# The first unit's projections in plain f32, earlier branch hints, and the last stores from ScalarE, in a gated-linear-attention plus mixture-of-heads kernel

## The chip, the cores and the metric

The kernel runs on 1 core of one Trainium2 chip. The metric is the device time of one execution in microseconds (us). Before the change the median of three runs is 321.53 us.

## The reference, cut to what matters

Two layers run one after the other. The first is gated linear attention over 4 batches, 8 heads, 768 steps, head size 48; its output, transposed, is the input `x` of the second, an attention with four experts.

```python
for t in range(S):                         # S = 768, per batch and head, state is 48 x 48
    state = alpha[:, :, t, :, None] * state + np.einsum('bhd,bhe->bhde', k[:, :, t], v[:, :, t])
    y[:, :, t] = np.einsum('bhd,bhde->bhe', q[:, :, t], state)
x = y.transpose(0, 2, 1, 3).reshape(B, S, H * D)         # 4 x 768 x 384
logits = x @ w_gate                        # top 2 of 4 experts, softmax of their logits: w
for e in range(E):                         # 4 experts, 64 columns each
    q, k, v = x @ wq[e], x @ wk[e], x @ wv[e]
    a = causal_softmax(q @ k.T / sqrt(64))
    out += (weight of e, 0 where not chosen) * (a @ v @ wo[e])
```

## The kernel before

**Chunks and units.** The first layer works on 24 chunks of 128 steps (six to a batch). For chunk `n`, VectorE runs two scans over alpha (`prep_r`, `prep_c`: the products of alpha from the chunk's end and from its start) and scales k and q by them. TensorE then forms k times q for the 8 heads (`gla_a`, L528), ScalarE or VectorE copies that out of PSUM under a causal mask (tile `ms`), TensorE transposes k (`gla_t`, L555) and adds to the state (`gla_u`, L573), and `gla_y` (L619) makes the chunk's output, already transposed, in PSUM. `check(n)` lets ScalarE take the sum of squares of alpha's products (L510); it guards against overflow. Three chunks are a unit `u` (384 rows of x); there are 8 units.

**Two f32r halves.** The second layer multiplies each operand as a pair of f32r tensors, a rounded one and the remainder: `xh`, `xl` for x, `wqk_h`, `wqk_l` and so on for the weights. ScalarE writes the first by a copy, VectorE the second by a subtraction, and each product is three matmuls. The weights arrive raw in two tiles of the pool `at` (`wqk`; `wv` and `wo` share one), which attention uses later, and are split once (`split_hi`, `split_lo`).

**Projections.** For the units 1 to 7, `proj` (L652) makes q and k of a pair of experts for all 384 columns at once. The first unit is done chunk by chunk instead, so that TensorE has work early: `projp` (L869) for 128 columns of q and of k (18 matmuls), `vproj` (L672) for v and the gate logits (9 matmuls). Then come scores (`score`, L730), softmax on VectorE and ScalarE, `norm` on GpSimd (L767), transposes (`transp`, L785), a times v (`av`, L822) and the output product (`outp`, L848), whose copy ScalarE makes (tile `ot`, L854) and whose store SyncE issues (L856).

**What sets the order.** `Plan.op` records every step with its engine, a modelled duration and its reads and writes. `Plan.schedule` places the steps by a list scheduler: of the steps that could start about now on an engine it takes the one that stands first in the table `TURN`, on TensorE preferring one that keeps the array's tiling (`MODE`: rows halved, columns split, or the full array). `Plan.emit` then writes them out, so each engine's order is fixed when the kernel is built. In the gaps that the plan sees before the array's first full load, `warm` (L1078) inserts dummy matmuls.

**The end.** A flag `cnt`, known long before the end, tells whether the overflow guard held. At the end every engine loads it and branches past a second, exact program that is not run. A hint to the instruction fetcher stands on each engine behind its anchor, the last step that started more than `HINT` = 9 us ahead of the plan's end (only steps whose function returns an instruction can be anchors):

```python
            if x is not None and o["start"] < self.end - HINT:
                self.anchor[o["eng"]] = x
...
        with tc.issue_after(pl.anchor[x].ins):
            tc.mark_branch_hint_location("exact", "LikelyTaken", [e.engine])
    good = nc.values_load(cnt, min_val=0, max_val=P * NG, skip_runtime_bounds_check_because="a count of P * NG flags")
    with tc.If(good < P * NG, label="exact"):
```

Of the kernel before, what the change touches and what calls it, by code (L numbers as in the profile page):

```python
# [56 lines left out]
HINT = 9.0  # L57
TURN = (
# [24 lines left out]
)  # L83
MS_ACT = 3
PIECE = 0.066
QB = 3
N128 = 0.066
# [7 lines left out]
class Plan:  # L95
# [180 lines left out]
    def emit(self, warm=None):  # L276
        pe, warming = ISSUE, True
        for i in self.order:
# [8 lines left out]
            if x is not None and o["start"] < self.end - HINT:  # L287
                self.anchor[o["eng"]] = x
# [3 lines left out]
def tile_gla_moe(ctx: ExitStack, tc: tile.TileContext, qk_d, al_d, v_d, wqk_d, wv_d, wo_d, nat_d, vn_d, out_d):  # L292
# [83 lines left out]
    def build(pl, first_pass):  # L376
        op = pl.op

# [220 lines left out]
        def gla_y(n):  # L599
# [23 lines left out]
            if not first:  # L623
                r += whole(("S", n))
            op("PE", occ, occ + 0.17, f, r=r, pe="py",
               w=whole(("py", n)), use=[("xh", u), ("xl", u)])
# [10 lines left out]
            op("V", *vec(384), fl, r=whole(("py", n)) + [(("xh", u), g)], w=[(("xl", u), g)])  # L637

# [19 lines left out]
        def split(src, c0, n, key, d0, part):  # L658
            cs, ds = slice(c0, c0 + n), slice(d0, d0 + n)
            op("A", *act(n), lambda T: A.activation(T(key)[:, 0, ds], T(src)[:, cs], AF.Copy),  # L660
               r=whole(src), w=[(key, (0, part))])
            op("V", *vec(n), lambda T: V.tensor_tensor(T(key)[:, 1, ds], T(src)[:, cs], T(key)[:, 0, ds].bitcast(F32),
                                                       OP.subtract),
               r=[(src, None), (key, (0, part))], w=[(key, (1, part))])

        def vproj(u, i):
            def f(T):
# [522 lines left out]
```

## Time and profile before

| | us |
|---|---|
| median of 3 runs (lowest, highest) | 321.53 (321.21, 327.66) |
| the profiled execution, its own time | 321.4 |
| its span, first to last instruction | 319.7 |
| TensorE busy | 309.8 (97%) |
| VectorE busy | 242.2 (76%) |
| ScalarE busy | 229.1 (72%) |
| GpSimd busy | 120.2 (38%) |

The profiled execution is 0.1 us below the median, and 1.7 us of it lie outside the span. Busy TensorE time counts each matmul from its start to a modelled end, so neighbours overlap and waits shorter than a matmul's tail don't show. PE is TensorE (PEld its weight loads), DVE VectorE, ACT ScalarE, POOL GpSimd, SP SyncE; a q behind a name is its sequencer.

### The profile page before, as it was taken

To read this page: it belongs to the slowest core of one execution; us is meant where nothing else is said; L and a number is where in the kernel's file an instruction comes from. 1 tells how busy PE (TensorE), PEld (TensorE's weight loads), DVE (VectorE), ACT (ScalarE), POOL (GpSimd) and SP (SyncE) were. 2 spreads that over 40 slices of the span, in tenths; PEclk is the share of its full clock that TensorE was granted. 3 is DMA by queue.
4 is the path that set the end of the run, shared out by engine and by line. 5 is a ranking of instruction groups with operands and counts; after the bars stand their busy time and mean duration, and the time that the engine had idled before them with its cause. 6 is when DMAs were issued, how large, how long until landed. Compare 5 with 4: busy or idle time off the path is not lost. (4 is left out here: it accounts for less than half of the span.)

```text
span 319.7 us, 9830 instructions
## 1 busy us (share of the span) xinstructions
PE 309.8 (97%) x3861; PEld 275.3 (86%) x3861; DVE 242.2 (76%) x708; ACT 229.1 (72%) x594; POOL 120.2 (38%) x177
## 2 busy tenths in 40 slices
PE   8989999999999999999999999999999999999991
PEld 6779998979999879898989899798899978888791
DVE  5999879999999999989999978447674364269430
ACT  0967567867799946869759969577785687669851
POOL 5253206504516510454805452501742060506420
PEclk9999999999999999999999999999999999999998
DMA  7998616313633084312333330240000100010201
GB/s 187 334 255 224 205 54 177 118 72 102 211 101 107 6 247 141 91 51 86 101 111 101 98 92 3 92 139 28 3 2 27 49 3 3 25 49 3 75 29 57
DMA packets 14198, 30.82 MB, mean 96 GB/s; under 512 B 1664, under 2 KB 4960, under 8 KB 14144
## 3 DMA queue, kind: packets, MB, share of 16 engines
q1 hardware_dynamic: 14144, 30.12, 31.4%
q8 instruction: 32, 0.52, 0.7%
q14 instruction: 22, 0.18, 0.2%
HBM read 25.39 MB, written 4.72 MB: 94 GB/s over the span
## 5 line engine op out<-in xcount | busy, mean ns | idle before, releaser
L767 POOL TENSOR_SCALAR a<-a,cf,gw 128x128 f32<-128x128 f32 (+5 forms) x96 | 77.9, 826 | 64.9 <-DVE cf L761 23.1
L748 ACT ACTIVATE a<-a,mx 128x128 f32<-128x128 f32 (+5 forms) x96 | 63.4, 664 | 11.0 <-DVE mx L739 10.9
L739 DVE CUSTOM_DVE_ANT_0 a<-g,cm 128x384 f32<-128x384 f32 (+3 forms) x96 | 47.0, 528 | 5.7 <-PE g L730 4.1
L799 ACT ACTIVATE at<-g 128x512 f32<-128x512 f32 (+3 forms) x124 | 48.8, 463 | 1.7 <-PE g L785 1.4
L785 PE MATMUL g<-ident,a 128*128 128x128 f32 x336 | 45.4, 276 | 0.0
L785 PEld LDWEIGHTS g<-ident,a 128*128 128x128 f32 x336 | 37.9, 141 | 3.1 <-issue 1.2
L822 PE MATMUL g<-at,vg 128*64 128x384 f32 (+2 forms) x324 | 39.5, 391 | 0.0
L730 PE MATMUL g<-k,q 64*128 64x256 f32 (+3 forms) x384 | 37.0, 331 | 0.0
L544 POOL TENSOR_SCALAR_AFFINE_SELECT ms<-ms 128x512 f32<-128x512 f32 x27 | 21.8, 815 | 38.6 <-ACT ms L540 38.3
L822 PEld LDWEIGHTS g<-at,vg 128*64 128x64 f32 x324 | 22.4, 137 | 15.9 <-issue 10.8
L619 PE MATMUL g<-ms,vt 128*32 128x128 f32 x768 | 33.0, 274 | 0.0
L730 PEld LDWEIGHTS g<-k,q 64*128 64x128 f32 x384 | 29.5, 185 | 3.1 <-issue 0.5
L467 DVE TENSOR_TENSOR_SCAN al<-al,d1r 112x516 f32<-112x516 f32 (+1 forms) x25 | 30.5, 1224 | 1.6 <-POOL mask L433 1.6
L590 POOL TENSOR_TENSOR C<-C,ev 112x192 f32<-112x192 f32 x16 | 11.0, 688 | 50.9 <-DVE C L588 49.6
L490 DVE TENSOR_TENSOR_SCAN al<-al,d1c 112x516 f32<-112x516 f32 (+1 forms) x25 | 30.1, 1207 | 0.0
L652 PE MATMUL g<-xh,wqk_h 128*128 128x384 f32 x84 | 29.9, 356 | 0.0
L510 ACT ACTIVATE al<-al 112x1033 f32<-112x1033 f32 x24 | 25.7, 1071 | 4.2 <-DVE qk L498 1.9
L652 PE MATMUL g<-xh,wqk_l 128*128 128x384 f32 x84 | 28.3, 336 | 0.0
L652 PE MATMUL g<-xl,wqk_h 128*128 128x384 f32 x84 | 28.2, 336 | 0.0
L528 PE MATMUL g<-qk 48*128 48x128 f32 x384 | 26.0, 279 | 0.0
L528 PEld LDWEIGHTS g<-qk 48*128 48x128 f32 x384 | 23.2, 187 | 1.7 <-issue 0.7
L619 PE MATMUL g<-qk,S 112*32 112x128 f32 x480 | 24.2, 272 | 0.0
(100 smaller groups left out, 682.0 us busy)
## 6 DMA issues: line engine op xcount, KB each, us to landing
qk<-in_qk_dram SPq DMA_DIRECT2D x24, 448.0 KB, 4.2
vt<-in_v_dram SPq DMA_DIRECT2D x25, 256.0 KB, 4.2
al<-in_al_dram SPq DMA_DIRECT2D x24, 226.2 KB, 3.3
out_dram<-ot SPq DMA_DIRECT2D x24, 192.0 KB, 1.9
at<-in_wqk_dram SPq DMA_DIRECT2D x1, 768.0 KB, 9.0
qk<-in_qk_dram SPq DMA_DIRECT2D x2, 224.0 KB, 4.1
at<-in_wvg_dram SPq DMA_DIRECT2D x1, 390.0 KB, 7.6
at<-in_wo_dram SPq DMA_DIRECT2D x1, 384.0 KB, 9.3
```

The lines of the kernel that those rows point to most:

```text
L467: V.tensor_tensor_scan(backwards(al[0:P, AW + c0 - 1:AW + c1 - 1]), backwards(al[0:P, c0:c1]), d1r[0:P, sl].rearrange("p a w -> p (a w)"), ...
L490: V.tensor_tensor_scan(c, c, T(("d1c", n))[0:P, sl].rearrange("p a w -> p (a w)"), 0.0, OP.mult, OP.max)
L528: PE.matmul(T(("pa", n, s))[:, C * p:C * p + C], t[r:r + D, p, C:2 * C], t[r:r + D, p, 0:C], start=True, stop=True, tile_position=(r, 0))
L619: PE.matmul(py[32 * j:32 * j + 32, k], l, r, start=(i == 0), stop=(i == len(parts) - 1), tile_position=(0, 32 * j))
L652: PE.matmul(pj[:, :W3], w[:, kt, cs], x[:, kt, :], start=(i == 0), stop=(i == 8))
L730: PE.matmul(T(sk[e])[:, :w], q[r, x, ts], k[r, y, c0:c1], start=(m == 0), stop=(m == 2), tile_position=(64 * e, 0))
L739: V.tensor_tensor_reduce(T(ak[e])[:, c0:c1], T(sk[e])[:, :w], cm[:, m0:m0 + w], -1.0, mx[:, 0:1] if x else BIG, OP.add, OP.min, accum_out= ...
L748: A.activation(a[:, 0:n], a[:, 0:n], AF.Exp, bias=T(mk)[:, e, len(pieces) - 1:len(pieces)], scale=-1.0, accum_out=T(("sm", u))[:, ix:ix + 1])
L767: G.tensor_scalar(a[:, 0:n], a[:, 0:n], T(ck_)[:, e:e + 1], T(("gw", u))[:, i, eg:eg + 1], op0=OP.mult, op1=OP.mult)
L785: PE.transpose(pt[:, 128 * (j - j0):128 * (j - j0) + 128], a[:, 128 * j:128 * j + 128], ident)
L799: A.activation(dst, src, AF.Copy)
L822: PE.matmul(py[64 * e:64 * e + 64, lo:n1], v[:, j % 3, 64 * eg:64 * eg + 64], at[e][:, at_off(j) + lo:at_off(j) + n1], start=(j == 0), sto ...
```

## The change

Four edits, and a new table `TURN` with them:

1. For the first unit, ScalarE copies each chunk's x as plain f32 into a tile of the pool `at`, `x32`, in place of `xh`; `xl` falls away. `vproj` and `projp` of this unit multiply x32 by the raw weights in plain f32: 3 matmuls in place of 9, and 6 in place of 18. The factor 1/8 of q moves from the weights to the copy out of PSUM (`scale`). The weights are split after the first unit's steps in the source.
2. `MS_ACT` goes from 3 to 0: for the first three chunks too, half of the masked copy is one VectorE multiplication, in place of a ScalarE copy and a GpSimd select.
3. `HINT` becomes a value for each engine: 9 for TensorE as it was, 120 for VectorE and ScalarE, 60 for GpSimd, 200 for SyncE.
4. The last two stores are issued by ScalarE.

```diff
-HINT = 9.0
+HINT = {"PE": 9.0, "V": 120.0, "A": 120.0, "G": 60.0, "S": 200.0}
 TURN = (
-    5, 17, 3, 30, 13, 72, 1, 4, 117, 15, 6, 154, 142, 59, 65, 61, 8, 93, 84, 223, 180, 68, 56, 97, 123, 29, 52, 102,
+    215, 75, 5, 3, 42, 289, 74, 30, 19, 90, 221, 119, 64, 23, 81, 48, 225, 40, 94, 1, 21, 49, 12, 44, 65, 220, 2,
...
-MS_ACT = 3
+MS_ACT = 0
...
-            if x is not None and o["start"] < self.end - HINT:
+            if x is not None and o["start"] < self.end - HINT[o["eng"]]:
...
+            if plain and u == 0:
+                def fx(T):
+                    A.activation(x32(T)[:, :, 128 * g:128 * g + 128],
+                                 T(("py", n))[:, 0:W3].rearrange("p (k t) -> p k t", k=3), AF.Copy)
+                op("A", *act(384), fx, r=whole(("py", n)), w=[(("at", -3), g)])
+                return
...
+            def f32(T):
+                for kt in range(3):
+                    PE.matmul(T(("pv", u, i))[:, 0:260], x32(T)[:, kt, 128 * i:128 * i + 128], wv[:, kt, :],
+                              start=(kt == 0), stop=(kt == 2))
...
+            if u == NU - 1 and i:
+                op("A", 0.36, 0, lambda T: A.dma_start(out_d[b, t0:t0 + 128, :], T(("ot", u, i))),
+                   r=whole(("ot", u, i)), dma=196608)
+            else:
+                op("S", 0.06, 0, lambda T: SY.dma_start(out_d[b, t0:t0 + 128, :], T(("ot", u, i))),
+                   r=whole(("ot", u, i)), dma=196608)
...
                     for kt in range(3):
-                        for w, x in ((wqk_h, xh), (wqk_h, xl), (wqk_l, xh)):
-                            PE.matmul(pj[:, 128 * which:128 * which + 128], w[:, kt, col], x[:, kt, cs],
-                                      start=(m == 0), stop=(m == 8))
-                            m += 1
+                        PE.matmul(pj[:, 128 * which:128 * which + 128], wqk[:, kt, col], x32(T)[:, kt, cs],
+                                  start=(kt == 0), stop=(kt == 2))
...
-            split(("pj", u, pair, i), 0, 128, ("q", u, pair), 128 * i, i)
+            split(("pj", u, pair, i), 0, 128, ("q", u, pair), 128 * i, i, isc)
...
             gla_y(n)
-            if n == 0:
-                split_hi(1)
-                split_lo(2)
             vproj(0, n)
             if n == 0:
-                split_hi(0)
-                split_lo(0)
-                split_lo(1)
                 constants3()
...
-        split_lo(3)
+        split_hi(1)
+        split_hi(0)
+        for x in range(4):
+            split_lo(x)
```

On TensorE, from the second chunk's transposes up to the first projections (tiles g are the eight PSUM banks; numbers tell buffers apart), before:

```order
L555 MATMUL g_67<-ident,qk_76 128x112 x4
...
L528 MATMUL g_68<-qk_76 128x128
L528 MATMUL g_69<-qk_76 128x128
...
L619 MATMUL g_70<-ms_90,vt_79 32x128 x16
L573 MATMUL g_63<-vt_80,kt_89 64x48
...
L672 MATMUL g_64<-wv_h,xh_96 128x260
L672 MATMUL g_64<-wv_l,xh_96 128x260
L672 MATMUL g_64<-wv_h,xl_98 128x260
```

and after:

```order
L618 MATMUL g_67<-ms_90,vt_79 32x128 x16
L554 MATMUL g_68<-ident,qk_76 128x112 x4
L527 MATMUL g_69<-qk_76 128x128
L527 MATMUL g_70<-qk_76 128x128
...
L679 MATMUL g_63<-at_137,at_138 128x260 x3
L890 MATMUL g_65<-at_138,at_136 128x128 x6
L890 MATMUL g_64<-at_138,at_136 128x128 x6
L572 MATMUL g_66<-vt_80,kt_89 64x48
```

The first chunk's output product (L619, now L618) has moved ahead of the second chunk's transposes and scores, and the second chunk's state product (L573, now L572) behind the first projections.

On ScalarE, from the first chunk's masked copy on, before:

```order
L540 ACTIVATE ms_90<-g_64 128x512
L540 ACTIVATE ms_90<-g_65 128x512
L558 ACTIVATE kt_89<-g_67 128x448
L408 ACTIVATE wv_h<-at_137 128x780
L595 ACTIVATE S_94<-C_92 48x4x48 x2
L510 ACTIVATE al_72,acc<-al_72 112x1033
L404 ACTIVATE wqk_h<-at_136 128x3x256
L405 ACTIVATE wqk_h<-at_136 128x3x256
L409 ACTIVATE wo_h<-at_137 128x768
L629 ACTIVATE xh_96<-g_70 128x3x128
```

and after:

```order
L539 ACTIVATE ms_90<-g_65 128x512
L594 ACTIVATE S_94<-C_92 48x4x48 x2
L407 ACTIVATE wv_h<-at_137 128x780
L637 ACTIVATE at_138<-g_67 128x3x128
L557 ACTIVATE kt_89<-g_68 128x448
L509 ACTIVATE al_72,acc<-al_72 112x1033
```

The copy of x (L629, now L637) stands behind one weight copy in place of four, and one copy of a masked half is gone from ScalarE.

At ScalarE's end, after:

```order
L873 ACTIVATE ot_144<-g_66 128x384
L876 DMA out_dram<-ot_144 128x384
L873 ACTIVATE ot_145<-g_70 128x384
L876 DMA out_dram<-ot_145 128x384
L1104 TENSOR_LOAD cnt
L1105 COMPARE_AND_BRANCH
```

The two issues of stores (L876) are new here; the load of the flag and the branch stand behind them. On SyncE, three steps stand between the last hint and the flag's load before; now 45 stand there, and on ScalarE 184 in place of 7, on VectorE 256 in place of 4; GpSimd's hint stands 35 steps ahead of it in place of 33.

## Rows read from the trace of the kernel before

**Rows 1.** Busy time by stage: stretch, its length, then each engine.

```profile
18.00:313.00 295.00, 294.92 (x3694) 263.63 (x3694) 228.73 (x686) 219.06 (x577) 113.78 (x155) 1.00 0.29 87
...
40.00:200.00 160.00, 160.00 (x2149) 145.62 (x2149) 147.74 (x405) 125.08 (x326) 65.72 (x87) 1.00 0.34 103
```

**Rows 2.** Timeline of TensorE: start, us, instruction; in brackets idle time before it.

```profile
14.90 1.08 PE L619 MATMUL g<-ms,vt 128*32 128x128 f32 x32
16.12 0.64 PE L573 MATMUL g<-vt,kt 128*64 128x48 f32 x16
18.01 0.40 PE L672 MATMUL g<-wv_h,xh 128*128 128x260 f32 x1 [1.25 <-ACT xh L629]
```

**Rows 3.** Timeline of ScalarE, the weights' first copy and the first x.

```profile
12.72 0.85 ACT L408 ACTIVATE wv_h<-at 128x780 fp32r<-128x780 f32 x1
...
17.48 0.47 ACT L629 ACTIVATE xh<-g 128x384 fp32r<-128x384 f32 x1
```

**Rows 4.** Timeline of GpSimd: the two selects of the first chunk's mask.

```profile
11.55 1.74 POOL L544 TENSOR_SCALAR_AFFINE_SELECT ms<-ms 128x512 f32<-128x512 f32 x2 [2.11 <-ACT ms L540]
```

**Rows 5.** Timeline of VectorE, the second chunk.

```profile
10.33 1.23 DVE L490 TENSOR_TENSOR_SCAN al<-al,d1c 112x516 f32<-112x516 f32 x1
...
12.11 0.68 DVE L498 TENSOR_TENSOR qk<-qk,al 112x512 f32<-112x512 f32 x1
```

**Rows 6.** Groups of VectorE: busy us, mean ns of one, then idle before.

```profile
L537 DVE TENSOR_TENSOR ms<-g,mask 128x512 f32<-128x512 f32 x21 | 14.1, 685 | 8.2 <-PE g L528 8.2
```

**Rows 7.** Landing of the second chunk's v, issued at 6.7 us.

```profile
DMA to landing us min/median/max: 9.3/9.3/9.3
```

**Rows 8.** Timeline of TensorE: one block of projections and what follows.

```profile
19.55 0.22 PE L869 MATMUL g<-xh,wqk_h 128*128 128x128 f32 x1
...
23.51 0.57 PE L555 MATMUL g<-ident,qk 112*128 112x112 f32 x4
...
24.40 1.11 PE L528 MATMUL g<-qk 48*128 48x128 f32 x16
25.44 0.43 PE L619 MATMUL g<-ms,vt 128*32 128x128 f32 x8
...
27.12 0.67 PE L573 MATMUL g<-vt,kt 128*64 128x48 f32 x16
```

**Rows 9.** Hints: durations in ns, first and last start in us.

```profile
L1186 POOLq BRANCH_PREFETCH_HINT  x1: 52/52/52, 237.3 to 237.3; - x1
...
L1186 PEldq BRANCH_PREFETCH_HINT  x1: 45/45/45, 305.5 to 305.5; - x1
```

**Rows 10.** The line of the branch: branches and each engine's first instruction behind.

```profile
L1088 SPq EVENT_SEMAPHORE  x8: 17/17/17, 317.8 to 318.3; - x8
L1088 POOLq COMPARE_BRANCH  x1: 65/65/65, 305.3 to 305.3; - x1
L1088 POOLq EVENT_SEMAPHORE  x1: 17/17/17, 307.9 to 307.9; - x1
...
L1088 PEldq COMPARE_BRANCH  x1: 408/408/408, 312.2 to 312.2; - x1
L1088 PEldq EVENT_SEMAPHORE  x1: 51/51/51, 313.3 to 313.3; - x1
L1088 ACTq COMPARE_BRANCH  x1: 68/68/68, 314.2 to 314.2; - x1
...
L1088 ACTq EVENT_SEMAPHORE  x1: 17/17/17, 317.3 to 317.3; - x1
```

**Rows 11.** Timeline of ScalarE: its last copy.

```profile
313.34 0.49 ACT L854 ACTIVATE ot<-g 128x384 f32<-128x384 f32 x1 [0.55 <-PEq L1088]
```

**Rows 12.** The last store: its issue in ns, and its landing.

```profile
L856 SPq DMA_DIRECT2D out_dram<-ot x1: 333/333/333, 313.9 to 313.9; - x1
...
DMA to landing us min/median/max: 3.1/3.1/3.1
```

**Rows 13.** Loads of the flag, durations in ns.

```profile
L1087 ACTq TENSOR_LOAD <-cnt x1: 731/731/731, 313.4 to 313.4; - x1
```

More of the change, by code (lines that the diff above doesn't have):

```diff
@@ L377, in build @@
         op = pl.op
+        plain = first_pass
         def load_al(n, p0=0, np=4):
@@ L625, in gla_y @@
             op("PE", occ, occ + 0.17, f, r=r, pe="py",
-               w=whole(("py", n)), use=[("xh", u), ("xl", u)])
+               w=whole(("py", n)), use=[("at", -3)] if plain and u == 0 else [("xh", u), ("xl", u)])
             def fh(T):
@@ L635, in fl, with x32 @@
                                 T(("xh", u))[:, :, 128 * g:128 * g + 128].bitcast(F32), OP.subtract)
+            if plain and u == 0:
[4 more added lines that the diff above has]
+                return
             op("A", *act(384), fh, r=whole(("py", n)), w=[(("xh", u), g)])
             op("V", *vec(384), fl, r=whole(("py", n)) + [(("xh", u), g)], w=[(("xl", u), g)])
+        def x32(T):
+            return T(("at", -3))[:, 0:3 * W3].rearrange("p (k t) -> p k t", k=3)
         def xs(u):
@@ L656, in proj, with split @@
             split(("pj", u, pair, which), 0, W3, ("k", b, pair) if which else ("q", u, pair), W3 * hf * which, 3 * hf * which)
-        def split(src, c0, n, key, d0, part):
+        def split(src, c0, n, key, d0, part, scale=1.0):
             cs, ds = slice(c0, c0 + n), slice(d0, d0 + n)
-            op("A", *act(n), lambda T: A.activation(T(key)[:, 0, ds], T(src)[:, cs], AF.Copy),
+            op("A", *act(n), lambda T: A.activation(T(key)[:, 0, ds], T(src)[:, cs], AF.Copy, scale=scale),
                r=whole(src), w=[(key, (0, part))])
-            op("V", *vec(n), lambda T: V.tensor_tensor(T(key)[:, 1, ds], T(src)[:, cs], T(key)[:, 0, ds].bitcast(F32),
-                                                       OP.subtract),
+            op("V", *vec(n), lambda T: V.scalar_tensor_tensor(
+                T(key)[:, 1, ds], T(src)[:, cs], scale, T(key)[:, 0, ds].bitcast(F32), op0=OP.mult, op1=OP.subtract)
+                if scale != 1.0 else V.tensor_tensor(
+                T(key)[:, 1, ds], T(src)[:, cs], T(key)[:, 0, ds].bitcast(F32), OP.subtract),
                r=[(src, None), (key, (0, part))], w=[(key, (1, part))])
         def vproj(u, i):
+            def f32(T):
+                for kt in range(3):
+                    PE.matmul(T(("pv", u, i))[:, 0:260], x32(T)[:, kt, 128 * i:128 * i + 128], wv[:, kt, :],
+                              start=(kt == 0), stop=(kt == 2))
             def f(T):
@@ L674, in f @@
                         m += 1
-            op("PE", 1.08, 1.25, f, pe="pv", r=[(("xh", u), i), (("xl", u), i)] + whole(("wv_h",), ("wv_l",)),
-               w=whole(("pv", u, i)), use=[("vg", u)])
+            if plain and u == 0:
+                op("PE", 1.31, 1.48, f32, pe="pv", r=[(("at", -3), i), (("at", -1), 0)],
+                   w=whole(("pv", u, i)), use=[("vg", u)])
+            else:
+                op("PE", 1.08, 1.25, f, pe="pv", r=[(("xh", u), i), (("xl", u), i)] + whole(("wv_h",), ("wv_l",)),
+                   w=whole(("pv", u, i)), use=[("vg", u)])
             op("A", *act(260), lambda T: A.activation(T(("vg", u))[:, i, :], T(("pv", u, i))[:, 0:260], AF.Copy),
@@ L731, in f @@
                                       tile_position=(64 * e, 0))
-                occ = 3 * (0.013 + w / 2400 if w > 128 else N128)
+                occ = 3 * max(0.11 + 0.006 * (w > 128), 0.014 + w / 2400)
                 op("PE", occ, occ + 0.17, f, pe="sc", r=[(("q", u, pair), (x, i if u == 0 else 0)) for x in (0, 1)]
@@ L855, in outp @@
                r=whole(("po", u, i)), w=whole(("ot", u, i)))
-            op("S", 0.06, 0, lambda T: SY.dma_start(out_d[b, t0:t0 + 128, :], T(("ot", u, i))),
-               r=whole(("ot", u, i)), dma=196608)
+            if u == NU - 1 and i:
+                op("A", 0.36, 0, lambda T: A.dma_start(out_d[b, t0:t0 + 128, :], T(("ot", u, i))),
+                   r=whole(("ot", u, i)), dma=196608)
+            else:
+                op("S", 0.06, 0, lambda T: SY.dma_start(out_d[b, t0:t0 + 128, :], T(("ot", u, i))),
+                   r=whole(("ot", u, i)), dma=196608)
         def projp(u, pair, i):
@@ L862, in f @@
             def f(T):
-                xh, xl, pj = T(("xh", u)), T(("xl", u)), T(("pj", u, pair, i))
+                pj = T(("pj", u, pair, i))
                 for which in (0, 1):
                     col = slice(256 * which + 128 * pair, 256 * which + 128 * pair + 128)
-                    m = 0
                     for kt in range(3):
-                        for w, x in ((wqk_h, xh), (wqk_h, xl), (wqk_l, xh)):
-                            PE.matmul(pj[:, 128 * which:128 * which + 128], w[:, kt, col], x[:, kt, cs],
-                                      start=(m == 0), stop=(m == 8))
-                            m += 1
-            op("PE", 18 * PIECE, 18 * PIECE + 0.17, f, pe="pj", r=[(("xh", u), i), (("xl", u), i)] + whole(("wqk_h",), ("wqk_l",)),
+                        PE.matmul(pj[:, 128 * which:128 * which + 128], wqk[:, kt, col], x32(T)[:, kt, cs],
+                                  start=(kt == 0), stop=(kt == 2))
+            op("PE", 1.32, 1.49, f, pe="pj", r=[(("at", -3), i), (("at", -2), None)],
                w=whole(("pj", u, pair, i)), use=[("k", 0, pair), ("q", u, pair)])
-            split(("pj", u, pair, i), 0, 128, ("q", u, pair), 128 * i, i)
+            split(("pj", u, pair, i), 0, 128, ("q", u, pair), 128 * i, i, isc)
             split(("pj", u, pair, i), 128, 128, ("k", 0, pair), 128 * i, i)
```

2 lines of the change are left out of this document (removed), and 46 rows, old and new, of the table TURN.

## The prediction

> **What bounds the kernel now.** I read the busy times by stage first. From 18 us to 313 us TensorE is busy for 294.92 of 295 us at the full clock [rows 1], and the list of waits names none for TensorE after 24 us. In between VectorE is busy for 147.7 of 160 us [rows 1]: close behind, but behind. So the time is: when TensorE's dense stretch begins, how much work is in it, and what comes after its last matmul. The timeline of TensorE gives the beginning. Its first projection starts at 18.01 us after 1.25 us of idle time that ended with ScalarE's copy of x, although the output product that x is copied from ran at 14.90 us [rows 2]. The copy waited in ScalarE's queue: it started at 17.48 us, behind the weights' copies, as the order has it [rows 3]. The rest is the tail: the last copy ends at 313.8 us [rows 11], and the span at 319.7 us.
>
> **The start.** The change takes the weights' split out of the way of the first projections. I place the new order by durations of the old rows. Chunk 0 is prepared as before, so ScalarE begins as early as it did. In place of two selects on GpSimd, 1.74 us for both from 11.55 us on [rows 4], one is left: done at about 12.5 us. The other half is a VectorE multiplication at 0.69 us [rows 6], behind the second chunk's scan of 1.23 us [rows 5], which now stands ahead of the multiplication of its k and so ends at about 10.9 us: done at 11.6 us. The output product can then start at 12.6 us in place of 14.90 us. It takes 1.05 us with its change of tiling (four groups at 0.21 us, below, and 0.2 us). The second chunk's transposes and scores, now behind it, take 0.57 and 1.04 us [rows 8]; the multiplications they need end near 13.4 us (11.6, a state sum, and twice 0.68 us [rows 5]). The copy of x, 0.47 us, runs on ScalarE behind one weight copy of 0.85 us [rows 3] and is done at 14.3 us, before the scores are. So the first projection starts at about 15.3 to 15.4 us: **2.6 us earlier**. Ends: 1.5 us, if the second chunk's data, now behind the first chunk's v on the same queue, lands 1 us later than I take; 3.1 us, if y starts as soon as the multiplication is done. In exchange the second chunk's state product, 0.64 us [rows 2] and 0.1 us for the tiling, is now inside the dense stretch: **+0.7 us**. Its v landed 9.3 us after an issue at 6.7 us [rows 7], and now lands after the third chunk's q and k as well, by the same rate 1.7 us later, at 17.7 us; it is wanted at 19.5 us.
>
> **The projections.** One block of 36 small f32r matmuls takes from 19.55 to 23.51 us, 3.96 us or 0.110 us each [rows 8]; three blocks make 11.9 us. A plain f32 matmul on the full array isn't in the trace, but f32 on parts of it is. Eight of them (x16: each shows as two instructions) in side-by-side pairs take 1.04 us from 24.40 to 25.44 us, with a change of tiling behind, so at most 0.21 us a pair at 0.2 us for the change; 28 in groups of four take 1.68 us, again 0.21 us a group [rows 8]. A pair and a group of four cost the same, so the parts run together and one matmul costs 0.21 us for 128 columns whatever its width. That gives 36 x 0.21 = 7.6 us, with a margin for starts 7.8 us: **-4.1 us**. By columns a `vproj` of 3 x 260 comes to 3 x 0.43 = 1.3 us; the old one takes 1.54 us at first, with a stall [rows 2, 8], and by the step of 0.110 us no less than 1.0 us later on: three together 0, between -0.3 and +0.7 us. **0**.
>
> **The new order of the rest.** Counted over the whole order, TensorE changes its tiling 85 times in place of 77, none of the eight more before the first projection. From rows 8, a change costs up to 0.2 us and takes the place of a step of 0.1 us or none: +0.8 to +1.6 us, **+1.0 us**. Waits that the new order makes I can't read from the old trace. The old dense stretch has almost none, and placing the first 20 us after 15.4 us by hand as above leaves TensorE waiting once, for the copy of the second chunk's x, by about 0.1 us, because ScalarE first has the three weight copies that are still to be made, and the q and k of two pairs. Both ends: 0, and 2 us if VectorE falls behind; **+0.3 us**. VectorE itself loses three remainders of x and gains three masks at 0.69 us [rows 6], about nothing in sum; the mask and the split of the weights now cover each other's queue, and without that slack each us on VectorE would be one on TensorE.
>
> **The tail.** ScalarE's branch comes at 314.2 us and its next instruction at 317.3 us, 3.1 us later; SyncE is back at 317.8 us; TensorE's branch costs 1.1 us [rows 10]. SyncE then steps through two rounds of waits and the engines meet, which leads to 319.7 us. After the change SyncE issues its last store some 6 us before the end, so its branch is over early. On ScalarE the issue, 0.33 us [rows 12], and the load, 0.73 us [rows 13], now follow the copy one after the other: the branch comes at 1.15 us after the copy's end in place of 0.35 us, and with 3.1 us for it ScalarE is back 4.4 us after the copy. SyncE waits for the store's landing, 3.1 us after its issue [rows 12], and then needs its second round, 0.5 us: 3.8 us after the copy, so ScalarE is the later of the two. The meeting takes another 0.7 us, so the tail is 5.2 us in place of 5.8 us: **-0.6 us**. Do the earlier hints help? GpSimd's hint stood at 237.3 us already, 68 us ahead of its branch, and GpSimd still came back 2.6 us after it [rows 9, 10], later than its own last work ended. Only TensorE, hinted 6.7 us ahead, was quick. So earliness alone didn't do it, and I count nothing for it. [...]
>
> **The sum.** -2.6 + 0.7 - 4.1 + 0 + 1.0 + 0.3 - 0.6 = -5.3 us. From the profiled execution's 321.4 us that is 316.1 us; the median lies 0.1 us higher, so **316.2 us**, 1.7% faster. 2%, about what a measurement of this kernel can tell from no change, would be 315.1 us.
>
> **Rivals.** *The hints work*: TensorE's does, and with a block of instructions still to be fetched between hint and branch the others may. Then ScalarE is back 2 us sooner and SyncE's 3.8 us set the end, or 1 us less if the store lands sooner from ScalarE's queue: another 0.7 to 1.7 us, **315.0 us**. For: TensorE; against: GpSimd. Chance 0.22. *VectorE becomes the bound*: it has 12 us of idle time in the 160 us from 40 us on [rows 1], and TensorE comes 2.6 us sooner with 4 us less of its own work for VectorE to hide behind. If VectorE's chain of scans, masks and splits paces the first 40 us, what the start gained goes: 316.2 + 2.6 = **318.8 us**. Against it: by my placing it holds for 20 us, and outside those 160 us VectorE is busy for 81 of 135 us [rows 1], time enough to catch up. Chance 0.18. *Slower than before*: a hint fetched early takes the place of the block that the engine needs next. Then ScalarE, VectorE and GpSimd each stall once in mid-program for what a missed branch costs, 3.1 us on ScalarE, 2.6 us on GpSimd [rows 10], and VectorE's taken halfway at 2.9 us, with TensorE waiting behind them: 316.2 + 8.6 = **324.8 us**. It decides as soon as two of the three fall on TensorE's path, since 5.3 us are then used up. Against it: GpSimd went on working after its early hint. Chance 0.04. The forecast itself has 0.55, and 0.01 is left over.
>
> **How the numbers follow.** The range goes from 313.9 us (working hints and a start 3.1 us earlier) to 318.8 us (the pace of VectorE), and leaves out the slower case and the ends beyond. Faster by over 2%: half of the first rival and a quarter of the forecast, 0.25. Slower by over 2% would take over 327.9 us: 0.02. Within 2%: 0.73.
>
> **What would show it.** Right: a first projection (the new line with 260 columns) near 15.4 us with no idle time of 1.25 us ahead of it; small plain f32 instructions 0.11 us apart, two to a matmul; TensorE dense to about 308 us; SyncE's branch well before the end, ScalarE's branch with 3 us behind it. Wrong: waits of TensorE on VectorE or ScalarE between 15 and 60 us, a f32 step other than 0.11 us, a branch of ScalarE that takes 1 us, or a stall in mid-program behind a hint.

## The result, and the profile after

| | before | after |
|---|---|---|
| median (lowest, highest), us | 324.6 (321.21, 328.09) | 316.83 (316.07, 317.55) |
| executions | 4 | 4 |
| ratio of comparable executions | | 0.9858, 95% interval 0.9817 to 0.99 |
| profiled execution, its span, us | 321.4, 319.7 | 317.55, 315.8 |

The change makes the kernel faster by 1.4%, which is 4.6 us of the 321.53 us that stood as the time before. Executions at a lowered clock (0.97 to 0.98 granted on average, against 0.99 and more) are left out of every ratio here; the profile of one experiment, `tail_only`, is of such an execution, so that only short stretches of it are read. The profiled execution after is the slowest of its four: its span is 3.8 us shorter than before (315.82 us against 319.66).

The timeline of TensorE gives the start (start, us, instruction; idle time ahead would stand in brackets):

```profile
12.70 1.08 PE L618 MATMUL g<-ms,vt 128*32 128x128 f32 x32
...
14.25 1.16 PE L527 MATMUL g<-qk 48*128 48x128 f32 x16
15.34 1.58 PE L679 MATMUL g<-at,at 128*128 128x260 f32 x6
16.76 2.84 PE L890 MATMUL g<-at,at 128*128 128x128 f32 x24
19.53 0.67 PE L572 MATMUL g<-vt,kt 128*64 128x48 f32 x16
...
25.09 1.48 PE L679 MATMUL g<-at,at 128*128 128x260 f32 x6
26.41 1.50 PE L890 MATMUL g<-at,at 128*128 128x128 f32 x12
...
309.08 0.34 PE L867 MATMUL g<-wo_h,yl 128*128 128x384 f32 x1
```

The first projection starts at 15.34 us in place of 18.01 us, with no idle time ahead [rows 2]. A chunk's block of small projections, 24 instructions of plain f32, takes 2.77 us from 16.76 to 19.53 us in place of 3.96 us [rows 8]. The dense stretch, from the first projection to the start of the last matmul, is 293.74 us; before it is 294.91 us, from 18.01 us [rows 2] to 312.92 us. The windows view of that stretch after (stretch, length, then busy us of TensorE, its weight loads, VectorE, ScalarE, GpSimd, then the clock) shows 0.36 us of idle time on TensorE:

```profile
15.34:309.08 293.74, 293.38 (x3667) 259.67 (x3665) 232.54 (x689) 221.78 (x580) 113.33 (x154) 1.00 0.32 90
```

The line of the branch, after (engine, instruction, ns, first and last start in us):

```profile
L1105 SPq EVENT_SEMAPHORE  x8: 17/17/17, 307.4 to 314.4; - x8
L1105 POOLq COMPARE_BRANCH  x1: 65/65/65, 302.1 to 302.1; - x1
L1105 POOLq EVENT_SEMAPHORE  x1: 17/17/17, 303.4 to 303.4; - x1
L1105 SPq COMPARE_BRANCH  x1: 70/70/70, 304.7 to 304.7; - x1
L1105 DVEq COMPARE_BRANCH  x1: 84/84/84, 308.1 to 308.1; - x1
...
L1105 DVEq EVENT_SEMAPHORE  x1: 21/21/21, 308.7 to 308.7; - x1
...
L1105 ACTq COMPARE_BRANCH  x1: 68/68/68, 313.5 to 313.5; - x1
L1105 ACTq EVENT_SEMAPHORE  x1: 17/17/17, 314.0 to 314.0; - x1
```

The time from an engine's branch to the instruction behind it, which was 3.1 us on ScalarE [rows 10], is 0.5 us now; on VectorE it is 0.6 us, on GpSimd 1.3 us in place of 2.6 [rows 10], on SyncE still 2.7 us. And the timeline of ScalarE at the end:

```profile
308.46 0.49 ACT L873 ACTIVATE ot<-g 128x384 f32<-128x384 f32 x1 [1.02 <-PE g L867]
308.98 2.97 ACTq L876 DMA_DIRECT2D out_dram<-ot  x1
312.05 0.49 ACT L873 ACTIVATE ot<-g 128x384 f32<-128x384 f32 x1 [3.10 <-issue]
312.57 0.34 ACTq L876 DMA_DIRECT2D out_dram<-ot  x1
```

The first of ScalarE's two issues takes 2.97 us, where one took 0.33 us on SyncE [rows 12], and the last copy of the kernel, whose matmul was done at 309.4 us, waits behind it. ScalarE is back from its branch at 314.0 us; the last store lands at 314.43 us, and the last of SyncE's eight waits starts at 314.4 us, so at the end it is the landing that the kernel waits for.

Where the 3.8 us come from, worked out from the start times of the matmuls in both traces: each interval between two starts is put down to the first one's kind if both are of one kind, otherwise to a change of tiling or to a change of kind in the same tiling (the latter is part of "all the rest"). Positive is longer after.

```
start of the first projection             18.01 -> 15.34    -2.67 us
dense stretch                            294.91 -> 293.74   -1.17 us
    small projections                     11.97 ->  7.59      -4.38
    vproj, all units                      25.30 -> 25.42      +0.12
    state products                         7.71 ->  8.21      +0.50
    70 -> 77 changes of tiling            14.11 -> 16.10      +1.98
    all the rest                                              +0.61
last matmul's start to the end             6.75 ->  6.75    0.00 us
```

These are terms of one profiled execution each. Over the nine kernels with the changed order that were profiled (`after` and the experiments on it, `old_order` not among them) the first projection starts between 14.7 and 15.6 us, and the dense stretch takes 293.4 to 294.1 us; so a term is good to some half a microsecond.

### The profile page after: what moved, and what is told of

Same layout as the page of the kernel before. It is cut to its first block, busy times and chain, and to the rows that moved or that the text cites. A ratio compares the mean times of both kernels' runs of the same rounds, so it can differ in the third digit from the quotient of the medians.

```text
span 315.8 us, 9736 instructions
## 1 busy us (share of the span) xinstructions
PE 307.5 (97%) x3809; PEld 270.4 (86%) x3809; DVE 243.9 (77%) x708; ACT 228.7 (72%) x591; POOL 119.1 (38%) x174
## 4 chain that ended last, share of the span: by engine, by line
PE 94%; DVE 2%; ACT 1%; ACTq 1%; issue 1%; POOL 0%; POOLq 0%
PE g L660 14%; PE g L804 12%; PE g L841 12%; PE g L618 11%; PE g L749 10%; PE g L867 8%; PE g L527 7%; PE g L687 7%; PE g L572 3%; PE g L1095 3%; PE g L554 2%; PE g L890 2%; PE g L679 1%; ACTq L876 1%; DVE al L466 0%
## 5 line engine op out<-in xcount | busy, mean ns | idle before, releaser
L786 POOL TENSOR_SCALAR a<-a,cf,gw 128x128 f32<-128x128 f32 (+5 forms) x96 | 80.7, 854 | 77.0 <-DVE cf L779 19.6
L767 ACT ACTIVATE a<-a,mx 128x128 f32<-128x128 f32 (+5 forms) x96 | 63.3, 661 | 12.2 <-DVE mx L758 11.6
L804 PE MATMUL g<-ident,a 128*128 128x128 f32 x336 | 46.1, 276 | 0.1
L841 PEld LDWEIGHTS g<-at,vg 128*64 128x64 f32 x324 | 21.7, 137 | 16.9 <-issue 13.6
L618 PE MATMUL g<-ms,vt 128*32 128x128 f32 x768 | 33.2, 275 | 0.0
L543 POOL TENSOR_SCALAR_AFFINE_SELECT ms<-ms 128x512 f32<-128x512 f32 x24 | 17.3, 722 | 41.8 <-ACT ms L539 41.7
L618 PE MATMUL g<-qk,S 112*32 112x128 f32 x480 | 24.2, 272 | 0.0
```

The costliest lines, as they stand in the source:

```text
L618: PE.matmul(py[32 * j:32 * j + 32, k], l, r, start=(i == 0), stop=(i == len(parts) - 1), tile_position=(0, 32 * j))
L767: A.activation(a[:, 0:n], a[:, 0:n], AF.Exp, bias=T(mk)[:, e, len(pieces) - 1:len(pieces)], scale=-1.0, accum_out=T(("sm", u))[:, ix:ix + 1])
L786: G.tensor_scalar(a[:, 0:n], a[:, 0:n], T(ck_)[:, e:e + 1], T(("gw", u))[:, i, eg:eg + 1], op0=OP.mult, op1=OP.mult)
L804: PE.transpose(pt[:, 128 * (j - j0):128 * (j - j0) + 128], a[:, 128 * j:128 * j + 128], ident)
L841: PE.matmul(py[64 * e:64 * e + 64, lo:n1], v[:, j % 3, 64 * eg:64 * eg + 64], at[e][:, at_off(j) + lo:at_off(j) + n1], start=(j == 0), sto ...
```

## The experiments

Eleven kernels, each timed beside the kernel before. In the table "issue" is that of ScalarE's first store; "fetch" tells whether a fetch of 8 KB of ScalarE's instructions began within 0.8 us of that issue's start (the trace lists DMAs of the kind "instruction" on queue q14, 20 of 8 KB each in `after`; which engine one belongs to is the author's reading, from its time and from the count of instructions); "branch" is the time from ScalarE's branch to its next instruction; "tail" is from the last matmul's start to the end of the span. The numbers of instructions count every record of the engine's trace from 0, waits included.

In `shift_many` the fetches put down to ScalarE began when it had started 319, 447, 576 and 700 instructions, 124 to 129 apart, and in `after` at 192, 313, 445, 567 and 704, 121 to 137 apart. A block below is 128 instructions, the author's estimate from that spacing. Where an engine's count enters the next block it is said to cross; the last crossings ahead of the branch are taken at ScalarE's number 703 and SyncE's number 79, because these start late: by 0.3 us the copy at 703 (1.32 us of idle time ahead of it in `warm_queue`, 1.02 us ahead of the same copy, there number 702, in `after`), by 0.4 us number 79 (0.44 us behind the end of the instruction ahead in `after`, its neighbours 0.04 to 0.06 us).

In `tail_only`, `shift_many` and `old_order` a fetch on q14 did begin 0.3 us after the first store's issue did; it is taken as VectorE's, because it comes 0.6 us behind VectorE's return from its branch, as one does in `after` and `warm_queue` too, and because ScalarE's count puts its own elsewhere.

| kernel | median us | ratio (95%) | number, issue us | queue used before | fetch | branch us | tail us |
|---|---|---|---|---|---|---|---|
| after | 316.83 | 0.9858 (0.9817, 0.99) | 703, 2.97 | no | yes | 0.48 | 6.7 |
| hint9 | 317.05 | 0.9851 (0.9833, 0.9868) | 703, 2.43 | no | yes | 0.49 | 6.2 |
| shift_one | 316.63 | 0.9836 (0.9813, 0.9859) | 704, 1.97 | no | yes | 0.49 | 6.0 |
| tail_only | 320.46 | 0.9962 (0.9949, 0.9976) | 699, 0.39 | no | no | 1.48 | 5.6 |
| shift_many | 316.22 | 0.9824 (0.9806, 0.9842) | 737, 0.39 | no | no | 0.49 | 5.0 |
| third_store | 315.85 | 0.981 (0.9794, 0.9826) | 695, 0.39 | no | no | 0.48 | 5.2 |
| warm_queue | 316.01 | 0.9823 (0.9805, 0.9841) | 704, 0.38 | yes | yes | 0.47 | 5.2 |
| warm_sp_hint | 315.94 | 0.9813 (0.9796, 0.9829) | 704, 0.38 | yes | yes | 0.47 | 5.2 |
| warm_no_hint | 316.3 | 0.9819 (0.9796, 0.9842) | 703, 0.38 | yes | yes | 2.57 | 5.5 |
| old_tail | 317.34 | 0.9866 (0.9849, 0.9883) | on SyncE | | | 1.43 | 6.3 |
| before_hints | 320.22 | 0.9951 (0.9931, 0.9971) | on SyncE | | | 1.78 | 5.8 |
| old_order | 323.05 | 1.0034 (1.0013, 1.0056) | 691, 0.39 | no | no | 0.49 | 4.9 |

The theory that the trace after suggested was that ScalarE's hint had worked after all, and that something new, the long issue, took back what it gave. Two rivals for the long issue: a price of the queue (Q), or a fetch (F).

**warm_queue.** The changed kernel with one small load more on ScalarE, in front of the plan's steps:

```diff
+    scr = consts.tile([1, 16], F32, name="scr")
+    A.dma_start(scr, nat_d[0][0:1, 0:16])
```

> The changed kernel with one more DMA: ScalarE, idle at the start, issues a load of 64 bytes into a scratch tile as its first instruction. In the changed kernel ScalarE's first issue of a store took 2.97 us (308.98 to 311.95 us), its second 0.34 us, and the last copy waited behind the first. Theory Q (queue): the 2.97 us is the price of the first DMA that ScalarE issues, whenever that is. Then the long issue moves to the start, where ScalarE waits for data until 7.5 us anyway, both stores at the end issue in some 0.34 us, the last copy starts about 2.6 us sooner, and the span falls from 315.8 to about 313.3 us. Theory F (fetch): the 2.97 us is a block of ScalarE's instructions that had to be fetched because the hinted target had taken its place. Then the early issue takes 0.4 us like SyncE's first, a stall of about 3 us stays near ScalarE's last copies (an instruction earlier or later), and the span stays at 315.8 us.

Measured: the early load issued in 0.54 us, the two stores in 0.38 and 0.55 us, and the span is 313.6 us. The gain is what Q expected, but the early issue was not long, which Q had asked for. F expected the stall to stay near the end; ScalarE's branch was as quick as in the changed kernel (0.47 us), so the hint worked, and no stall of 3 us stayed: F falls in this form. Timeline of ScalarE:

```profile
0.81 0.54 ACTq L1098 DMA_DIRECT2D scr<-in_nat_dram  x1
...
308.11 0.49 ACT L873 ACTIVATE ot<-g 128x384 f32<-128x384 f32 x1 [1.32 <-PE g L867]
308.63 0.38 ACTq L876 DMA_DIRECT2D out_dram<-ot  x1
309.12 0.49 ACT L873 ACTIVATE ot<-g 128x384 f32<-128x384 f32 x1 [0.51 <-PEq L1108]
309.64 0.55 ACTq L876 DMA_DIRECT2D out_dram<-ot  x1
```

**hint9.** The changed kernel with a `HINT` of 9.0 for every engine.

> The changed kernel with every hint again at 9 us ahead of the planned end, the stores still from ScalarE. Both theories: ScalarE's branch takes about 3.1 us as in the kernel before (0.48 us in the changed kernel). Theory Q: the first store's issue still takes about 3 us, so ScalarE comes back 2.6 us later and the span is about 318.4 us. Theory F: no hinted target has displaced a block, so the first store issues in about 0.4 us, the last copy ends 2.6 us sooner, the branch gives that back, and the span stays near 315.8 us.

Measured: both were wrong about the branch. It took 0.49 us with a hint at 303.5 us, 10 us ahead of it, as with one 124 us ahead; and the issue took 2.43 us. So the quick branch doesn't come from the hint's earliness, nor does the long issue. VectorE, whose hint now stands 9 us ahead of the planned end, behind the last fetch ahead of the branch that is put down to it (at 267.9 us in the changed kernel), took 2.8 us (308.4 to 311.2 us) in place of 0.6 us. From the line of the branch:

```profile
L1105 DVEq COMPARE_BRANCH  x1: 84/84/84, 308.4 to 308.4; - x1
...
L1105 DVEq EVENT_SEMAPHORE  x1: 21/21/21, 311.2 to 311.2; - x1
L1105 ACTq COMPARE_BRANCH  x1: 68/68/68, 313.2 to 313.2; - x1
L1105 ACTq EVENT_SEMAPHORE  x1: 17/17/17, 313.7 to 313.7; - x1
```

**old_tail.** The changed kernel, hints as in hint9, and the two stores back on SyncE.

> The changed kernel with the tail of the kernel before: all hints at 9 us, the last two stores from SyncE. First projection near 15.3 us and last matmul near 309.1 us, as in the changed kernel; after it the 6.8 us that the kernel before has from its last matmul's start at 312.9 us to its end. Span about 315.9 us: what the change gained is in the start and the dense stretch, and its tail is worth 0.1 us.

Measured: first projection at 14.7 us, last matmul at 308.4 us, tail 6.3 us, time 317.34 us. ScalarE's branch took 1.43 us. Start and dense stretch (293.72 us) carry nearly all of the gain; the new tail's share, 0.5 us between the medians, is not resolved by the intervals.

**tail_only.** The kernel before with `HINT` of the change and the branch `if u == NU - 1 and i` for the stores, nothing else.

> The kernel before with only the new hints and ScalarE's two stores: projections, masks and order as before. First projection at 18.0 us, last matmul at 312.9 us. Theory Q: the first store's issue takes 3 us, ScalarE's branch about 0.5 us, span about 319.6 us, no difference to before. Theory F: the same sum, since the stall of 3 us and the quick branch belong together.

Measured: 0.4% faster (interval 0.2 to 0.5%), where both theories expected nothing. ScalarE's branch took 1.48 us, where both expected 0.5 us. The first store, on an unused queue, issued in 0.39 us, the second in 1.18 us, which stays unexplained. Here the stores stand at numbers 699 and 702, ahead of ScalarE's number 703, where the next fetch falls by the count.

From these four came a new pair: the place (P: a store that stands at number 703) or the queue (Q).

**shift_one.** The changed kernel with two more copies on ScalarE, and with SyncE's hint at 240.

```diff
+            def fv(T):
+                for _ in range(2 if u == 3 and i == 0 and first_pass else 0):
+                    A.activation(T(("vg", u))[:, i, :], T(("pv", u, i))[:, 0:260], AF.Copy)
+                return A.activation(T(("vg", u))[:, i, :], T(("pv", u, i))[:, 0:260], AF.Copy)
```

> The changed kernel with one ScalarE instruction more in mid-program (a copy of the fourth unit's v made three times, which adds two copies and saves one separate wait), no early DMA on ScalarE; and SyncE's hint at 240 us ahead of the planned end in place of 200, so that it stands in front of SyncE's 79th instruction. In the traces so far ScalarE's instruction number 703 is the one that is late: the first store's issue in the changed kernel (2.97 us) and with the hints at 9 us (2.43 us), a copy that began 0.34 us late with the early load, the load of the flag 0.34 us late in the kernel before with the new tail, whose first store, number 699, issued in 0.39 us. Theory P (place): the 2.97 us belongs to the place, where a fetch of 8 KB also begins, and to a store standing there. Then the first store, now number 704, issues in 0.4 us, the copy in front of it begins about 0.3 us late, and the time falls as with the early load, from 316.8 to about 316.0 us. Theory Q (queue): the first DMA of an unused queue is slow; then it stays near 3 us and the time stays at 316.8 us. SyncE's branch: 2.7 us in the changed kernel. If a hint acts when its engine next crosses into the block of 128 instructions that holds the branch, it takes 0.5 us now; if not, 2.7 us again. It isn't on the path.

**warm_no_hint.** warm_queue without ScalarE's hint.

> The kernel with the early load on ScalarE, and ScalarE's hint left out, so that the first store is again ScalarE's instruction number 703. Theory P (place): the first store's issue takes 2.4 to 3 us although the queue has been used; ScalarE's branch has no hint and takes about 3 us; ScalarE comes back 5 us later than with the early load alone, at about 316.3 us, and the span is about 318 us. Theory Q (queue): the first store issues in 0.4 us, the branch takes about 3 us, ScalarE comes back at about 313.8 us, and the span is about 315.3 us.

Measured: with an unused queue the store at number 704 took 1.97 us, so it isn't the very place; with a used queue the store at 703 took 0.38 us. Timelines of ScalarE, shift_one, then warm_no_hint:

```profile
308.65 1.97 ACTq L879 DMA_DIRECT2D out_dram<-ot  x1
310.72 0.49 ACT L876 ACTIVATE ot<-g 128x384 f32<-128x384 f32 x1 [2.10 <-issue]
```

```profile
308.94 0.38 ACTq L876 DMA_DIRECT2D out_dram<-ot  x1
309.42 0.49 ACT L873 ACTIVATE ot<-g 128x384 f32<-128x384 f32 x1 [0.51 <-PE g L867]
```

P falls, and Q alone doesn't fit tail_only. Left was that both are needed (C): an unused queue, and ScalarE's fetch under way. Without its hint ScalarE's branch took 2.57 us, against 0.47 us in warm_queue, which differs in the hint alone: here the hint made it quick. The time hardly shows it: the tail is 0.3 us longer than in warm_queue and the medians are 0.3 us apart, within the intervals. Even so late ScalarE is not the last: it reaches its drain behind the branch at 313.5 us, SyncE its last one at 313.8 us. SyncE's branch took 0.5 us in shift_one, from 304.1 to 304.6 us.

**before_hints.** The kernel before with ScalarE's copies as in shift_one, but three extra, and SyncE's hint at 240; all others at 9.

> The kernel before, order and stores as they were, with two edits: SyncE's hint moved from 300 us to about 69 us, in front of SyncE's instruction number 79, and two ScalarE instructions more in mid-program, so that ScalarE's branch becomes number 704 in place of 702, with its hint 7 us ahead as it was. If a hint acts at the next crossing into a block of 128 instructions (number 79 on SyncE, 703 on ScalarE), SyncE's branch falls from 2.96 to about 0.5 us, ScalarE's from 3.15 to about 1.5 us (the fetch begins less than a microsecond ahead of the branch), and then the landing of the last store, at 317.0 us, sets the end: span about 318.4 us in place of 319.7, 0.4% faster. If hints act in another way, both branches stay at 3 us and so does the time. No loss is expected from the hint that stands 245 us early.

Measured: SyncE 0.48 us (315.14 to 315.62), ScalarE 1.78 us, span 318.4 us, 0.5% faster (0.3 to 0.7%). SyncE's 0.48 us is the number expected if a hint acts when its engine crosses into a new block; ScalarE's 1.78 us is longer than the 1.5 us expected, but far from 3.15 us. With several crossings behind the hint there is tail_only: ScalarE's hint stood 124 us ahead of the branch, and ScalarE entered new blocks at its numbers 447 and 575 in between, yet the branch took 1.48 us; the fetch at the last crossing, number 703, began 0.05 us ahead of the branch. So the two earlier crossings did not make that branch quick; that the last one ahead of the branch counts is the author's reading. From the line of the branch (SyncE's first instruction behind its branch is the first of the eight):

```profile
L1091 SPq EVENT_SEMAPHORE  x8: 17/17/17, 315.6 to 317.1; - x8
...
L1091 ACTq COMPARE_BRANCH  x1: 68/68/68, 314.0 to 314.0; - x1
...
L1091 SPq COMPARE_BRANCH  x1: 70/70/70, 315.1 to 315.1; - x1
L1091 ACTq EVENT_SEMAPHORE  x1: 17/17/17, 315.8 to 315.8; - x1
```

**shift_many.** The changed kernel with four extra copies of 8 columns in each chunk of the fourth to sixth unit, made as in shift_one; SyncE's hint stays at 200.

> The changed kernel with 34 ScalarE instructions more in mid-program (copies of 8 columns of v, made four times each in the fourth to sixth unit), no early DMA on ScalarE. The first store then stands some 34 places behind ScalarE's number 703, and the fetch of 8 KB that begins there is over some 8 us before the store. So far: an unused queue with that fetch at the store, 2.97, 2.43 and 1.97 us for the first issue; a used queue with the fetch at the store, 0.38 us twice; an unused queue without the fetch, 0.39 us once, in the kernel before with the new tail, whose second issue took 1.18 us. Theory Q (the unused queue alone): the first issue takes 2 to 3 us again, and the time is that of the changed kernel or the 0.1 us more that the copies cost. Theory C (an unused queue and a fetch under way): it takes 0.4 us, and the time falls to about 316.0 us, as with the early load. In both ScalarE's branch is quick, about 0.5 us, since its target was fetched long before.

**third_store.** The changed kernel with `if u == NU - 1:` in place of `if u == NU - 1 and i:`, so that ScalarE issues the last three stores.

> The changed kernel with the third-last store issued by ScalarE too, some 5 us ahead of the other two; no early DMA. Theory Q: that issue, near 303.5 us, is the first on the queue and takes 2 to 3 us; ScalarE's copies of transposed attention behind it come late, TensorE waits for them some 2 us, and the last two stores issue in 0.4 us each: time about that of the changed kernel, 316.8 us, since the stall is on the path in one place or the other. Theory C: all three issue in 0.4 us, the time falls to about 316.2 us.

Measured: in shift_many number 703 ran at 293.1 us, 16.5 us ahead of the first store. In both kernels the first issue on the unused queue took 0.39 us, C's number; the times are 316.22 and 315.85 us. The timelines of ScalarE, shift_many and third_store:

```profile
309.63 0.39 ACTq L879 DMA_DIRECT2D out_dram<-ot  x1
310.11 0.49 ACT L876 ACTIVATE ot<-g 128x384 f32<-128x384 f32 x1 [0.52 <-PE g L870]
```

```profile
303.22 0.39 ACTq L876 DMA_DIRECT2D out_dram<-ot  x1
...
308.41 0.34 ACTq L876 DMA_DIRECT2D out_dram<-ot  x1
308.93 0.49 ACT L873 ACTIVATE ot<-g 128x384 f32<-128x384 f32 x1 [0.55 <-PE g L867]
309.45 0.34 ACTq L876 DMA_DIRECT2D out_dram<-ot  x1
```

So the runs fill all four fields: unused queue with a fetch, 1.97 to 2.97 us (three kernels); unused without, 0.39 us (four, old_order below among them); used with, 0.38 us (three); used without, 0.34 us for most of the later stores, but 0.55 us in warm_queue, 0.61 us in warm_sp_hint and 1.18 us in tail_only. Issues of that size occur on SyncE's queue too, which is used from the start (0.3 to 0.4 us mostly, single ones up to 1.75 us, in old_order); none there reaches 1.97 us.

**warm_sp_hint.** warm_queue with SyncE's hint at 240.

> The kernel with the early load on ScalarE, and SyncE's hint at 240 us ahead of the planned end, so that SyncE's branch takes 0.5 us in place of 2.7. SyncE then waits for the landing of the last store in either case, so no difference to the early load alone is expected: about 316.0 us, the fastest version that the runs point to, with the last store's landing and 1.4 us behind it as its end.

Measured: 315.94 us, no difference to warm_queue, as expected: the first of SyncE's eight waits starts 7.7 us behind its branch either way (304.0 and 311.7 us in warm_queue, 304.3 and 312.0 us here). third_store, 315.85 us, has the lowest median of all kernels here, 1.9% below the kernel before; the intervals do not tell it from warm_sp_hint or warm_queue, nor from the change itself, whose interval reaches 1.8%; but the four kernels with a short issue and a quick branch all lie 0.3 to 0.5% below the change.

**old_order.** The change with the table `TURN` of before, each entry translated to the same step's new number.

> The changed kernel with the table of the kernel before, its entries translated to the same steps. The scheduler answers the other durations with an order of its own: from the first projection on TensorE changes its tiling 93 times, where the changed kernel does so 77 times and the kernel before 70 times. At 0.21 us for each (7 more changes cost 2.0 us in the trace of the changed kernel, all 77 together 16.1 us) the dense stretch is 3.4 us longer than the changed kernel's; at the 0.125 us for each that the prediction took it is 2.0 us longer. Start within 1 us of 15.3 us. Time about 319 to 320.5 us.

Measured: 323.05 us, slower than expected and slower than the kernel before. The first projection starts at 16.41 us and the dense stretch is 300.07 us, 6.3 us longer than the changed kernel's. Windows of it, and lines of the list of TensorE's waits that lie in it (us in total, times, longest):

```profile
16.41:316.48 300.07, 295.83 (x3654) 257.54 (x3653) 231.35 (x687) 219.64 (x577) 115.69 (x153) 1.00 0.30 87
```

```profile
PE g L888 <- ACT at L635: 1.7, 1, 1.7
...
PE g L747 <- DVE mx L756: 1.1, 1, 1.1
...
PE g L865 <- ACT ms L537: 0.5, 1, 0.5
```

TensorE is idle for 4.24 us of the stretch (300.07 less 295.83), against 0.36 us in the changed kernel, and busy 2.45 us longer. By the start times, as above, the intervals at a change of tiling take 5.86 us more, 2.46 us of it idle; the other 3.40 us are 0.21 us for each of the 16 more changes, as expected, and what was not expected is the idle time. In this order the cheap projections gained nothing: it has waits of TensorE that the new table keeps away, the longest for ScalarE's copy of a chunk's x. That every order not made for them would lose as much is not shown.

## Why the prediction was right or wrong

The time, 316.83 us, is 0.6 us above the forecast of 316.2 us and inside its range, but the forecast put its weight on "within 2%", taking 2% as what a measurement can tell from no change. That bound was far too wide: the interval of the ratio is 0.4% to either side, and 1.4% stands clear of it, so "within 2%" was the wrong call for a sum that said 1.7%. That the time lies so near is in part luck: in the profiled span the gain is 3.8 us where the sum said 5.3 us, and the profiled execution is the slowest of its four. By size the new order is furthest off, by 1.3 us; by mechanism the tail is wrong. Term by term:

- **The start, -2.6 us: right**, -2.67 us in this execution, and step by step. The mask's multiplication was done at 11.45 us (11.6 predicted), the select at 12.04 (12.5), the output product started at 12.70 (12.6), the copy of x ended at 14.34 (14.3), the first projection started at 15.34 us (15.3 to 15.4).
- **The moved state product, +0.7 us:** +0.50 us without its change of tiling. Right.
- **The projections, -4.1 us: right**, -4.38 us; two instructions of 0.11 us for each small f32 matmul. `vproj`, taken as 0: +0.12 us.
- **The new order, +1.0 us, and its waits, +0.3 us: too small.** The 7 more changes come with 1.98 us, 0.28 us each, where the term took 0.125 us for each of eight ("takes the place of a step of 0.1 us or none"); old_order's 0.21 us each shows that one price for a change does not fit every order. Another 0.6 us lies spread over the other kinds, the idle time of 0.36 us in it. Together these are 2.6 us in place of 1.3 us, and the dense stretch gained 1.2 us in place of 2.1 us.
- **The tail, -0.6 us: the step that failed.** It said that ScalarE's branch would still miss ("with 3.1 us for it") and that the store's issue would cost 0.33 us. The branch took 0.48 us, 2.6 us less; the first issue took 2.97 us, 2.6 us more, which the trace of before couldn't show, since ScalarE issued no DMA there. So the path was another too: it ran through the long issue and the last store's landing, not through ScalarE's branch. The tail did not move in the profiled execution (6.75 us both times), and by 0.5 us between the medians of old_tail and the change; that it came out within 0.6 us of the forecast is two errors that cancel. Where the issue is short (third_store, warm_queue), the tail is 5.2 us. The prediction's own terms, 1.15, 3.1 and 0.7 us, add up to 5.0 us after the copy and not to 5.2 us, so as written they give between -0.8 and -0.9 us.
- **"Earliness alone didn't do it" was right, its reason was not seen.** GpSimd's early hint [rows 9] stood some ten instructions behind the last fetch put down to GpSimd ahead of its branch, at 228.4 us. In the changed kernel it stands at 237.5 us, no earlier, but some ten instructions ahead of that fetch, at 239.8 us, and GpSimd was back 1.3 us after its branch, as soon as its own last work had ended. What the runs show is this: ScalarE's branch took 0.47 to 0.49 us where its hint stood ahead of its last crossing and the fetch there began 1.9 us or more ahead of the branch (hint9, shift_one, warm_sp_hint); 1.43 to 1.78 us where that fetch began 0.9 us ahead (old_tail), 0.05 us ahead (tail_only) or just behind the branch (before_hints); 2.57 us without a hint (warm_no_hint); and 3.15 us where the hint stood behind the last crossing (the kernel before). In that kernel ScalarE's branch was number 702, the fetch at the last crossing began at 261.7 us, and the hint stood at 307.2 us; two instructions more put a crossing between hint and branch, and in before_hints they brought the branch from 3.15 to 1.78 us. How a hint acts inside the fetcher no run shows.
- **The rivals.** "The hints work" came true on ScalarE (0.48 us), VectorE (0.6 us) and GpSimd (1.3 us), and its gain, for which it said 315.0 us, was held back by the long issue; the kernels freed of that reach 315.85 to 316.2 us, and there the quick branch has little to give: 0.3 us between the medians of warm_no_hint and warm_queue. "VectorE becomes the bound": no, 0.36 us of idle time on TensorE. "A hint takes the place of a needed block": no stall of that kind; the long issue looked like one, but in warm_queue the branch took 0.47 us and the issue 0.38 us.

**What stays open:** why an unused queue and a fetch under way make a long issue together. The long issues ended 1.7 to 2.2 us after the fetch put down to ScalarE began, and in the kernel before GpSimd, VectorE and ScalarE were back from their branches of 2.6 to 3.15 us 1.6 to 2.0 us after a fetch on q14 began. That the issue waits for that fetch to land is the author's guess from these like times; no run here separates it further, nor tells why the issue took 0.38 us on a used queue.

## What to carry to other kernels

Before moving the first DMA of an engine's queue to the end of a program, try an earlier issue by that engine, or a place for it away from the engine's instruction fetches: here the first store's issue took 0.38 or 0.39 us in place of 1.97 to 2.97 us, worth some 0.4% between the medians. For a branch hint, count instructions from the branch back to the last fetch of the engine, and look in the trace at how far ahead of the branch it begins: here ScalarE's branch took 0.47 us with that fetch behind the hint and 1.9 us ahead of the branch (warm_sp_hint), 1.43 us with 0.9 us (old_tail), and 3.15 us with the fetch ahead of the hint (the kernel before). A quick branch saves time only if nothing else ends as late: between warm_no_hint and warm_queue, 2.57 and 0.47 us, the medians are 0.3 us apart, within the intervals. A cheaper operation needs an order of its own: with the old table the same edits were 0.3% slower than no change.

## What the runs showed of the hardware

Instruction DMAs moved 8 KB each on q14 and 16 KB each on q8, as the third part of the page of the changed kernel shows (queue, packets, MB, share):

```profile
q8 instruction: 31, 0.51, 0.7%
...
q14 instruction: 20, 0.16, 0.2%
```

The author puts q14 down to ScalarE, VectorE, GpSimd and SyncE and q8 to TensorE, by times and counts of instructions.

ScalarE's copy at number 703 started 0.3 us late in warm_queue and shift_one (1.32 and 1.30 us of idle time ahead of it, against 1.02 us ahead of the same copy in the changed kernel), and SyncE's number 79 started 0.4 us late in the changed kernel. ScalarE's branch took 1.43 us in old_tail, 1.48 us in tail_only and 1.78 us in before_hints, where the fetch behind its hint began less than a microsecond ahead of the branch, or just behind it.
